# A chained attention and two gated FFNs: the second-last phase's out projection by seven quarter products, and the second FFN's input parts formed from the first one's output tiles

## The chip, the cores and the metric

One core of a Trainium2 chip. The metric is the device time of one execution in microseconds, the median of several runs.

## What is computed

```python
kv = einsum('bhsd,bhse->bhde', k, v)          # 8 x 8 x 576 x 64, float32
out = einsum('bhsd,bhde->bhse', q, kv)
x = out / sqrt(mean(out * out, -1) + 1e-6) * g_norm    # -> (4608, 512)
y = (sigmoid(x @ w_gate) * (x @ w_val)) @ w_out        # d_ff 1536
g = y @ w2_gate
z = (g * sigmoid(g) * (y @ w2_val)) @ w2_out           # (4608, 512)
```

All of it is float32; attention is linear, and two gated FFNs follow it.

## The kernel before

**Precision.** Every large product is made of rounded pieces (fp32r): an operand is split into a high part (a ScalarE copy) and a low part (a subtraction), and three products of the parts are added in PSUM. Weights are rounded and split on the chip as well; `rounded` (L377) is a chain of six operations, one on ScalarE and five on VectorE.

**Phases.** The 4608 tokens are nine blocks of 512 (`NBLK`). The hidden width of 1536 is twelve chunks of 128; a phase takes six of them for one FFN through all nine blocks. Phases 0 and 1 are FFN 1, phases 2 and 3 are FFN 2 (`PH`). In phase 0 the attention runs beside the first FFN's first half, in plain form. Phases 1 to 3 take the chunks in pairs, three steps a block (27 steps a phase), and make the gate and value products from seven quarter products instead of eight (`gv_win`, L686): 84 matmuls of 256 columns a step. The seven operands of x and of the weights (three quarters and four combinations of quarters, each in two parts) have to be formed first.

**Out products.** In phases 0 to 2 a step's out product is plain: 24 matmuls of 512 columns (`part_win`, L842), done after the next step's gv product. Only phase 3 (`WOUT`, L334) uses seven quarter products there too (`out_win`, L852): four products "early" after each step (24 matmuls of 256 columns), and three "late" ones over all three steps at the end of a block (54 matmuls). That needs h in seven operands: 11, T1, T3, T2 into two alternating places (`h_places`, L675), 21, 22, T4 into a place for each step. Each is a ScalarE copy and a GpSimd subtraction (`put`).

**x.** `x_steps` (L590) loads a block's x in four quarters of 256 KB, forms the seven operands (seven ScalarE copies, three VectorE and four GpSimd subtractions, four VectorE differences) one block ahead. Blocks alternate between a right-hand place and the arena on the left. FFN 1's output goes to DRAM (`xd[1, j]`, called yd in the trace) from `evac` (L991) in phase 1 and is loaded again in phase 2. There `keep` (L636) stores the fourteen parts of each block to `xc` in DRAM. Phase 3 loads these parts piece by piece into one place as the products of the last step before free them (`x_load`, L571, called in `product`, L721).

**Weights.** `stage` (L440) rounds a later phase's weights, forms their seven operands and stores them to `wd` in DRAM; `stage_pair` does the same for phase 3's out weights. `place` (L552) loads them in the last block before a phase, as the place of the old ones comes free (`put_place`, L1102).

**Order.** The order of PE, ScalarE, VectorE and GpSimd is written out by hand. Between products stands `tick()` (L1088; ten ticks a step), which takes thunks from queues: `att` attention, `xq` x steps, `kq` parts to keep, `wq` weights, `pq` staging. A queue paces its items by their due times (`Queue`, L1035). Phase 1's weights are staged until block 7 of phase 0, phase 2's in phase 1, phase 3's in phase 2 (`STAGED`, L1146). SP issues nearly all DMAs, in program order.

```python
721    def product(a, b, ps=None, more=False):
728        for e, w in enumerate(ws):
729            for n, (l, r) in enumerate(terms):
730                for kk in range(2):
731                    nc.tensor.matmul(ps[:, e], w[:, l, kk], xs[r // 5][:, r % 5, kk], ...)
732        if ph in WOUT and m + 2 == PH[ph][1] + PH[ph][2] and j + 1 < NBLK:
733            x_load(ph, j + 1, b)
```

Of the kernel before, what the change touches and what calls it, by code (L numbers as in the profile page):

```python
# [20 lines left out]
def attention_two_ffn(ctx: ExitStack, tc: tile.TileContext, q, k, v, g_norm, weights, out):  # L21
# [13 lines left out]
    P = 128  # L35
# [24 lines left out]
    H_AT, ARENA_AT, X_AFTER = 4 * LINE, LINE, 7 * LINE  # L60
    RIGHT, LEFT = {(1, 0): (0, LINE)}, {2: 4 * LINE}
    FIRST = {(0, 0): 5 * LINE}
# [10 lines left out]
    def open_left():  # L73
        lo_ctx.close()
        late["L"] = ctx.enter_context(tc.tile_pool(name="late_l", bufs=1, reuse_waits="tile"))
        for m in range(PH[1][1] + 2, PH[1][1] + 6):
            w_tile(0, m, 0)
        late["arena"] = shifted(late["L"], 11 * KB, F32R, ARENA_AT, "arena")

# [25 lines left out]
    for j in range(NBLK):  # L105
# [3 lines left out]
        xd[1, j] = dr.tile([P, KD, NB], F32, name=f"yd{j}")  # L109
# [224 lines left out]
    WOUT = (3,)  # L334
# [8 lines left out]
    def nop():  # L343
        pass

# [12 lines left out]
    def w_tile(f, m, c):  # L358
        d = wo if c == 2 else wgv
        if (f, m) not in d:  # L360
            ph, s = phase_of[f, m]
            pool = w0p if ph == 0 else late["R" if s < NRIGHT else "L"]
            if c == 2 and ph in WOUT:
                a = 3584 * (s // 2)
# [12 lines left out]
    def rounded(f, m, c, buf):  # L377
# [62 lines left out]
    def stage(f, m):  # L440
# [7 lines left out]
        e = m % 2  # L448
        paired = phase_of[f, m][0] in WOUT
# [18 lines left out]
        l0, o0, s0 = rounded(f, m - e, e, buf)  # L468
        l1, o1, s1 = rounded(f, m - e + 1, e, buf)
        l2, o2, s2 = rounded(f, m, 2, buf)  # L470
# [32 lines left out]
        if paired:  # L503
            return parts[0] + [parts[1][0], nop, nop] + parts[1][3:] + th + (stage_pair(f, m, buf, store, fl, hi, lo) if e else [])
# [10 lines left out]
    def stage_pair(f, m, buf, store, fl, hi, lo):  # L515
        Q, E = 2 * P, 14 * 2 * P
        l0, o0, s0 = rounded(f, m - 1, 2, buf)
        l1, o1, s1 = rounded(f, m, 2, buf)
# [14 lines left out]
        return [l0, l1, nop, nop] + o0 + o1 + [  # L533
# [18 lines left out]
    def place(f, m):  # L552
# [11 lines left out]
        return load_gv, load_o  # L564

# [10 lines left out]
    def x_tiles(ph, j):  # L576
        if (ph, j) not in xt:
            if PH[ph][3]:
                s = "RL"[((ph - 1) * NBLK + j) % 2]
                if ph in WOUT and j:  # L580
                    xt[ph, j] = x_tiles(ph, 0)
                elif s == "L":
                    xt[ph, j] = [late["arena"][:, i * 5 * DM:min(i * 5 + 5, 14) * DM].rearrange("p (c k a) -> p c k a", k=2, a=HB) for i in range(3)]
                else:
                    xt[ph, j] = [shifted(late[s], (10 - i // 2 * 2) * HB, F32R, (0, X_AFTER * (i // 2)), f"x{i}", f"x{i}").rearrange("p (c k a) -> p c k a", k=2, a=HB) for i in range(3)]
# [4 lines left out]
    def x_steps(ph, j):  # L590
# [20 lines left out]
        if ph in WOUT:  # L611
            return [lambda b=b: x_load(ph, j, b) for b in range(7)]

# [10 lines left out]
        def W(i, n, o, eng=nc.vector):  # L624
            return lambda: eng.tensor_tensor(out=X(o + 7), in0=st[i, n], in1=X(o).bitcast(F32), op=ALU.subtract)

        def D(o, a, b):
            return lambda: sub(st[o], st[a], st[b])
# [7 lines left out]
    def keep(ph, j, i):  # L636
        if j not in xc:
            xc[j] = dr.tile([P, 14 * DM], F32, name=f"xc{j}")
        t = x_tiles(ph, j)[i // 5][:, i % 5].rearrange("p k a -> p (k a)")
        nc.sync.dma_start(out=xc[j][:, i * DM:(i + 1) * DM], in_=t.bitcast(F32))  # L640
# [6 lines left out]
    h_all = shifted(hp_, 12 * HB, F32R, H_AT, "h").rearrange("p (b e s a) -> p b e s a", b=2, e=2, s=3)  # L647
    hp_.tile([P, 7 * LINE], F32, name="gap")
# [26 lines left out]
    def h_places():  # L675
        if not hw:
            raw = [wk.tile([P, 4, HB], F32R, tag="raw", name="he") for _ in range(2)]
            own = [shifted(late["R"], 4 * HB, F32R, w_shift(1, i, 2), "he", f"wo{i}").rearrange("p (c a) -> p c a", a=HB) for i in range(2)]
            hw["E"] = raw, own
            flat = h_all.rearrange("p a b c d -> p (a b c) d")  # L680
            far = [wk.tile([P, 2, HB], F32R, tag="xl", bufs=3, name="hl") for _ in range(3)]
            hw["L"] = [[flat[:, 6 * p + 2 * i:6 * p + 2 * i + 2] for i in range(3)] for p in range(2)] + [far]
            hw["n"] = 0
        return hw
# [600 lines left out]
```

## Time and profile before

| | us |
|---|---|
| median of 3 runs | 1784.44 (1781.6 to 1785.17) |
| the profiled execution, its time | 1781.64 |
| its span, first to last instruction | 1779.9 |
| PE busy | 1757.9 (99%) |
| DVE, ACT, POOL busy | 1060.0, 660.7, 683.2 |
| first gv product of phase 1, 2, 3 (chain of waits) | 549.9, 958.44, 1371.07 |

The profile shows one execution. The span leaves out what lies before the first and after the last instruction. PE's matmuls are pipelined, so busy time is no measure of its own limit. In the trace a matmul group is named by output and operands: `gv` is a gate/value product, `o` an out product, `he`, `h`, `hl` are the places of h's parts. `L341` and `L338` are the helpers `add` and `sub`.

### The profile page before, as it was taken

To read this page: it belongs to the slowest core of one execution; us is meant where nothing else is said; L and a number is where in the kernel's file an instruction comes from. 1 tells how busy PE (TensorE), PEld (TensorE's weight loads), DVE (VectorE), ACT (ScalarE), POOL (GpSimd) and SP (SyncE) were. 2 spreads that over 40 slices of the span, in tenths; PEclk is the share of its full clock that TensorE was granted. 3 is DMA by queue.
4 is the path that set the end of the run, shared out by engine and by line. 5 is a ranking of instruction groups with operands and counts; after the bars stand their busy time and mean duration, and the time that the engine had idled before them with its cause. 6 is when DMAs were issued, how large, how long until landed. Compare 5 with 4: busy or idle time off the path is not lost.

```text
span 1779.9 us, 31991 instructions
## 1 busy us (share of the span) xinstructions
PE 1757.9 (99%) x12358; PEld 1616.1 (91%) x12358; DVE 1060.0 (60%) x1754; ACT 660.7 (37%) x1349; POOL 683.2 (38%) x748
## 2 busy tenths in 40 slices
PE   7899999999999999999999999999999999999998
PEld 6788888888889999999999999999999999999998
DVE  6766566654335667676666666655553555555555
ACT  4664233333233333333333443443432433333332
POOL 1654445431012443343433444343441344444444
PEclk9999999999999999999999999999999999999999
DMA  9958796456336533434349855555568644343442
GB/s 286 285 164 230 221 227 161 132 142 237 106 108 257 187 129 103 142 107 137 125 145 397 294 188 183 185 190 189 190 237 313 214 131 131 131 131 131 131 131 72
DMA packets 274825, 320.40 MB, mean 180 GB/s; under 512 B 95856, under 2 KB 193392, under 8 KB 271984
## 3 DMA queue, kind: packets, MB, share of 16 engines
q1 hardware_dynamic: 259504, 305.24, 52.9%
q10 hardware_dynamic: 15168, 13.11, 2.4%
q8 instruction: 97, 1.59, 0.4%
q14 instruction: 56, 0.46, 0.1%
HBM read 191.14 MB, written 127.14 MB: 179 GB/s over the span
## 4 chain that ended last, share of the span: by engine, by line
PE 92%; DVE 3%; DMA 2%; issue 1%; ACT 1%; SPq 1%; POOL 1%; DVEq 0%; ACTq 0%
PE gv L731 43%; PE o L842 16%; PE gv L660 15%; PE o L828 8%; PE o L863 7%; PE ops L221 1%; PE kvps L171 1%; DMA raw<-in_moe_w_out_dram 0%; DMA qm<-in_q_dram 0%; PE xTp L268 0%; DVE u L341 0%; DVE pl L341 0%; SPq L118 0%; DMA pl<-pd 0%; DVE u L400 0%
## 5 line engine op out<-in xcount | busy, mean ns | idle before, releaser
L731 PE MATMUL gv<-x,wgv 128*128 128x256 f32 x4536 | 539.7, 279 | 0.4 <-DVE v L341 0.3
L731 PEld LDWEIGHTS gv<-x,wgv 128*128 128x128 f32 x4536 | 535.9, 188 | 3.2 <-DVE v L341 0.8
L660 PE MATMUL gv<-x,wgv 128*128 128x512 f32 x1296 | 313.8, 393 | 3.5 <-ACT x L275 2.4
L660 PEld LDWEIGHTS gv<-x,wgv 128*128 128x128 f32 x1296 | 240.3, 188 | 53.5 <-ACT x L275 2.9
L731 PEld LDWEIGHTS gv<-arena,wgv 128*128 128x128 f32 x2268 | 268.8, 188 | 3.0 <-DVE v L341 0.7
L731 PE MATMUL gv<-arena,wgv 128*128 128x256 f32 x2268 | 269.8, 279 | 0.1
L341 DVE TENSOR_TENSOR u<-u,gv 128x512 f32<-128x512 f32 x162 | 110.9, 684 | 244.8 <-PE gv L731 232.8
L719 POOL TENSOR_TENSOR h<-v,h 128x512 fp32r<-128x512 f32 x54 | 75.0, 1389 | 235.8 <-ACT h L715 235.6
L828 PE MATMUL o<-h,wo 128*128 128x512 f32 x648 | 161.9, 394 | 0.3 <-DVE h L338 0.3
L704 ACT ACTIVATE w<-v 128x256 f32<-128x256 f32 x81 | 33.9, 419 | 307.0 <-DVE v L341 307.0
L828 PEld LDWEIGHTS o<-h,wo 128*128 128x128 f32 x648 | 120.0, 188 | 25.1 <-DVE h L338 0.7
L719 POOL TENSOR_TENSOR h<-w,h 128x512 fp32r<-128x512 f32 x54 | 70.6, 1307 | 131.9 <-ACT h L715 129.9
L668 DVE TENSOR_TENSOR sg<-sg,gv 128x512 f32<-128x512 f32 x54 | 37.0, 684 | 112.1 <-PE gv L660 112.0
L842 PE MATMUL o<-h,arena 128*128 128x512 f32 x432 | 101.4, 390 | 0.0
L842 PE MATMUL o<-arena,h 128*128 128x512 f32 x432 | 101.4, 390 | 0.0
L842 PEld LDWEIGHTS o<-h,arena 128*128 128x128 f32 x432 | 79.8, 188 | 15.9
L842 PEld LDWEIGHTS o<-arena,h 128*128 128x128 f32 x432 | 79.8, 188 | 15.9
L775 POOL TENSOR_TENSOR he<-w,he 128x256 fp32r<-128x256 f32 x27 | 20.0, 742 | 182.1 <-ACT he L774 154.7
L863 PE MATMUL o<-arena,he 128*128 128x256 f32 x648 | 82.2, 281 | 0.0
L704 ACT ACTIVATE v<-g 128x256 f32<-128x256 f32 x81 | 33.9, 418 | 128.8 <-DVE g L341 128.8
L341 DVE TENSOR_TENSOR g<-u,gv 128x512 f32<-128x512 f32 x81 | 55.6, 687 | 41.4 <-PE gv L731 40.1
L863 PEld LDWEIGHTS o<-arena,he 128*128 128x128 f32 x648 | 79.0, 189 | 0.0
(145 smaller groups left out, 2601.0 us busy)
## 6 DMA issues: line engine op xcount, KB each, us to landing
wgv<-wd SPq DMA_DIRECT2D x18, 1792.0 KB, 10.0
x<-xc SPq DMA_DIRECT2D x126, 256.0 KB, 4.2
pl<-pd SPq DMA_DIRECT2D x80, 256.0 KB, 4.1
pd<-ye SPq DMA_DIRECT2D x72, 256.0 KB, 2.8
xc<-arena SPq DMA_DIRECT2D x70, 256.0 KB, 3.5
wd<-raw SPq DMA_DIRECT2D x63, 256.0 KB, 3.0
xc<-x SPq DMA_DIRECT2D x56, 256.0 KB, 3.6
raw<-in_moe_w_gate_dram SPq DMA_DIRECT2D x24, 512.0 KB, 4.6
```

Source lines behind the costliest of these rows:

```text
L171: nc.tensor.matmul(kvps[b][e * D:(e + 1) * D, hp, :D], lt, rt, start=(r == hp == 0), stop=(r == R and hp == NP - 1), skip_group_check=True)
L221: nc.tensor.matmul(ps[:, hp, :], t[:, hp, :], kvbd[2 * bp + (i > R)][:, hp, :], start=True, stop=True)
L341: nc.vector.tensor_tensor(out=out, in0=a, in1=b, op=ALU.add)
L660: nc.tensor.matmul(ps, w[:, e, a, kk, :], x[b][:, kk, :], start=(n == 0), stop=(n == 3 * KD - 1))
L668: nc.vector.tensor_tensor(out=sg, in0=sg, in1=bank[1], op=ALU.mult)
L704: nc.scalar.activation(o, t[:, 0], AF.Silu if f else AF.Sigmoid)
L719: nc.gpsimd.tensor_tensor(out=t[:, 1], in0=v, in1=t[:, 0].bitcast(F32), op=ALU.subtract)
L731: nc.tensor.matmul(ps[:, e], w[:, l, kk], xs[r // 5][:, r % 5, kk], start=(fresh and e == n == kk == 0), stop=(not more and e == 1 and n = ...
L775: nc.gpsimd.tensor_tensor(out=hs[z][:, 1], in0=x, in1=hs[z][:, 0].bitcast(F32), op=ALU.subtract)
L828: nc.tensor.matmul(ps, l, r, start=(fresh and t == 0), stop=(last and t == 2))
L842: nc.tensor.matmul(ps, l, r, start=(fresh and e == t == 0), stop=(last and e == 1 and t == 2))
L863: nc.tensor.matmul(ps[:, t], h[:, r, cs], w[:, Ax[a] + 7 * l], start=(start and t == n_ == 0), stop=(stop and t == 1 and n_ == 2), skip_gr ...
```

## The change

- `WOUT` becomes (2, 3). Phase 2's out products are formed as phase 3's are; `first_sums` adds them up into tiles and stores the partial sums. Phase 3's out weights are loaded by `place_seven`, the early pieces after each step of phase 2's last block, the late ones after the block.
- In phase 1 `evac` adds the out product to the partial sums in halves of 256 columns, and `comp_steps` forms FFN 2's x parts from these tiles and stores them to `xc`, from a new place `spare`; `yd`, `keep` and phase 2's `x_steps` go. Block 8's parts are formed in phase 2's first block, in the `xl` buffers. Every block of phases 2 and 3 loads its parts by `x_load`.
- The staging of phases 2 and 3 has a queue `rq` with due times in shares: half of phase 2's by the end of phase 0, the rest by block 5 of phase 1; a quarter of phase 3's before phase 2, the rest in phase 2. It rests from 12 ticks before phase 2 to 42 after its start. In it the last addition of `rounded` and the low parts go from VectorE to GpSimd.
- A tick takes at most one queued VectorE operation inside a gv product and two between out parts.
- h's 11 parts are issued before the seventh product, T1 to T2 after the first out part (`mid_h`), with tiles g, w0 and v in place of `ta` and `tb`. The alternating h places use `spare` in place of `raw` buffers.
- wgv is loaded in four pieces. Some addresses shift.

```diff
-    WOUT = (3,)
+    WOUT = (2, 3)
...
-    def rounded(f, m, c, buf):
+    def rounded(f, m, c, buf, eng=nc.vector):
...
         def o7():
-            add(st["u"], st["u"], st["s"])
-        return load, [o1, o3, o4, o5, o6, o7], st
+            eng.tensor_tensor(out=st["u"], in0=st["u"], in1=st["s"], op=ALU.add)
+        return load, [o1] + [V(z) for z in (o3, o4, o5, o6)] + [V(o7) if eng is nc.vector else o7], st
...
+        late_eng = nc.gpsimd if phase_of[f, m][0] > 1 else nc.vector
...
-        def lo(o, x, h, eng=nc.vector):
+        def lo(o, x, h, eng=late_eng):
...
         def load_gv():
-            nc.sync.dma_start(out=t, in_=wd[f, m][:, :E])
+            for a in range(0, E, E // 4):
+                nc.sync.dma_start(out=t[:, a:a + E // 4], in_=wd[f, m][:, a:a + E // 4])
...
+    def place_seven(f, m, what):
+        Q, E = 2 * P, 14 * 2 * P
+        for a, b in ((0, 1), (3, 6)) if what == "early" else ((1, 3), (6, 7)):
+            for l in range(2):
+                a_, b_ = a + 7 * l, b + 7 * l
+                t = w_tile(f, m, 2)[:, a_:b_].rearrange("p q a -> p (q a)").bitcast(F32)
+                nc.sync.dma_start(out=t, in_=wd[f, m][:, E + a_ * Q:E + b_ * Q])
...
-                if ph in WOUT and j:
-                    xt[ph, j] = x_tiles(ph, 0)
+                if ph in WOUT:
+                    xt[ph, j] = x_tiles(WOUT[0] - 1, NBLK - 1)
...
-    def keep(ph, j, i):
...
+    def comp_steps(j, st, buf):
+        z, th = {}, []
+        xc[j] = dr.tile([P, 14 * DM], F32, name=f"xc{j}")
+        def store(o):
+            nc.sync.dma_start(out=xc[j][:, o * DM:(o + 1) * DM], in_=z[o].rearrange("p k a -> p (k a)").bitcast(F32))
+        def H(i, n, o):
+            def run():
+                z[o] = buf()
+                nc.scalar.activation(z[o], st[i, n], AF.Copy)
+                store(o)
+            return run
+        def W(i, n, o, eng=nc.vector):
+            def run():
+                z[o + 7] = buf()
+                eng.tensor_tensor(out=z[o + 7], in0=st[i, n], in1=z[o].bitcast(F32), op=ALU.subtract)
+                store(o + 7)
+            return V(run) if eng is nc.vector else run
+        def D(o, a, b):
+            return V(lambda: sub(st[o], st[a], st[b]))
+        po = nc.gpsimd
+        return [H(0, 0, 0), W(0, 0, 0), D((0, 0), (0, 1), (0, 0)), H(1, 1, 2), W(1, 1, 2), D((0, 1), (1, 1), (0, 1)), H(0, 0, 3), W(0, 0, 3, po), nop, D((0, 0), (1, 1), (0, 0)),
+                H(0, 1, 5), W(0, 1, 5, po), nop, H(1, 0, 1), W(1, 0, 1), D((1, 0), (1, 0), (0, 0)), H(0, 0, 4), W(0, 0, 4, po), nop, H(1, 0, 6), W(1, 0, 6, po)]
...
-            if ph in WOUT and m + 2 == PH[ph][1] + PH[ph][2] and j + 1 < NBLK:
-                x_load(ph, j + 1, b)
+            after = (ph, j + 1) if j + 1 < NBLK else (ph + 1, 0)
+            if after[0] in WOUT and m + 2 == PH[ph][1] + PH[ph][2]:
+                x_load(*after, b)
...
+            def mid_h():
+                sub(g[:, 0], v[:, 0], w0[:, 0])
+                put("T1", g[:, 0])
+                sub(g[:, 1], v[:, 1], v[:, 0])
+                put("T3", g[:, 1])
+                sub(w0[:, 0], v[:, 1], g[:, 0])
+                put("T2", w0[:, 0])
 
             def late_h():
                 gated(w0[:, 1], w0[:, 1], u)
-                sub(tb[:, 1], w0[:, 1], ta[:, 1])
+                sub(v[:, 0], w0[:, 1], w0[:, 0])
                 put("22", v[:, 1])
                 put("21", w0[:, 1])
-                put("T4", tb[:, 1])
+                put("T4", v[:, 0])
...
+            def y4():
+                late("12", "21", st["c1"], all_m, False)
+                t = tile_("yt")
+                nc.scalar.activation(t, st["c1"], AF.Copy)
+                done(t, 0, 0)
+            def y5():
+                p = ps_o.tile([P, 2, HB], F32, tag="o", name="o")
+                late("S4", "22", p, all_m, True)
+                add(st["g"], st["g"], p)
+                done(st["g"], 0, 1)
+            def y6():
+                late("22", "T4", st["c7"], all_m, False)
+                add(st["u"], st["u"], st["c7"])
+                done(st["u"], 1, 0)
...
+        if ph + 1 == WOUT[0]:
+            a, k = divmod(i, 2)
+            for n in range(2):
+                t = part[ph, j, 2 * a + n]
+                add(t[:, k], t[:, k], ps[:, n * HB:(n + 1) * HB])
+            if i == 1:
...
+                th = comp_steps(j, {divmod(z, 2): part.pop((ph, j, z)) for z in range(4)}, buf)
+                for k, z in enumerate(th):
+                    kq.put(now[0] + (1 if j + 1 < NBLK else 13) + (0.75 if j + 1 < NBLK else 0.6) * k, [z], j)
+            return
...
+                if paced and t in on_vector:
+                    if not budget[0]:
+                        self.credit += n - z
+                        return
+                    budget[0] -= 1
...
-        if not first and not 0 <= now[0] - tick_of(1, 0, 0) < 13:
-            pq.pace(dt)
+        if not first and not 0 <= now[0] - tick_of(1, 0, 0) < 13 and not (-12 <= now[0] - tick_of(2, 0, 0) < 42 and rq.whole()):
+            (rq if pq.at == len(pq.items) else pq).pace(dt)
...
+    SHARES = {2: ((tick_of(1, 0, 0) - 1, 0.5), (tick_of(1, 5, 0), 1)), 3: ((tick_of(2, 0, 0) - 14, 0.25), (tick_of(2, NBLK - 1, 0) - 2, 1))}
...
+                    if j:
+                        kq.need(j - 1)
                     for z in range(4):
                         load_part(ph, j, z)
```

## Rows read from the trace of the kernel before

**Rows 1.** The page: busy us, share of the span, instructions, by engine

```profile
PE 1757.9 (99%) x12358; PEld 1616.1 (91%) x12358; DVE 1060.0 (60%) x1754; ACT 660.7 (37%) x1349; POOL 683.2 (38%) x748
```

**Rows 2.** Windows: length, busy us of PE, PEld, DVE, ACT, POOL; clock, DMA, GB/s

```profile
441.00:545.00 104.00, 104.00 (x461) 86.11 (x460) 42.73 (x66) 31.08 (x55) 10.92 (x10) 1.00 0.30 102
549.90:958.44 408.54, 408.00 (x2894) 382.06 (x2894) 276.48 (x440) 148.59 (x298) 155.91 (x125) 1.00 0.47 160
958.44:1371.07 412.63, 412.63 (x2918) 386.36 (x2918) 242.42 (x393) 163.40 (x324) 162.93 (x134) 1.00 0.63 224
1386.34:1740.91 354.57, 354.57 (x3027) 354.57 (x3026) 201.48 (x365) 116.11 (x298) 151.30 (x185) 1.00 0.42 136
```

**Rows 3.** The chain in order of time, phase 2: start us, us, what

```profile
1050.33 9.80 PE gv L731 x84
1060.13 5.47 PE o L842 x24
```

**Rows 4.** The chain in order of time, a block of phase 3

```profile
1396.15 2.80 PE o L863 x24
...
1408.74 2.88 PE o L863 x24
...
1422.12 8.51 PE o L863 x72
```

**Rows 5.** Timeline of POOL, DVE and PE in phase 3: start us, us

```profile
1486.63 1.02 POOL L775 TENSOR_TENSOR he<-ta,he 128x256 fp32r<-128x256 f32 x1 [0.88 <-ACT he L774]
...
1490.58 0.73 POOL L775 TENSOR_TENSOR h<-tb,h 128x256 fp32r<-128x256 f32 x1
...
1486.29 0.41 DVE L338 TENSOR_TENSOR ta<-v,ta 128x256 f32<-128x256 f32 x1
...
1487.07 0.86 DVE L338 TENSOR_TENSOR tb<-w,ta 128x256 f32<-128x256 f32 x1
...
1493.29 0.69 DVE L341 TENSOR_TENSOR v<-g,gv 128x512 f32<-128x512 f32 x1 [0.77 <-PE gv L731]
...
1487.43 9.96 PE L731 MATMUL gv<-x,wgv 128*128 128x256 f32 x84
```

**Rows 6.** Lines of the whole trace: busy us, mean ns of one

```profile
L341 DVE TENSOR_TENSOR u<-u,s 128x512 f32<-128x512 f32 x72 | 54.2, 753 | 1.0
...
L625 POOL TENSOR_TENSOR arena<-xl,arena 128x512 fp32r<-128x512 f32 x36 | 49.9, 1394 | 41.2 <-ACT arena L622 41.2
...
L477 POOL TENSOR_TENSOR s<-u 128x256 f32<-128x256 f32 x36 | 30.5, 848 | 117.8 <-DVE u L341 111.3 <-issue 5.2 <-PE o L842 1.4
...
L466 POOL TENSOR_TENSOR s<-s,raw 128x512 fp32r<-128x512 f32 x21 | 28.1, 1337 | 33.9 <-issue 31.4 <-POOL h L719 0.7 <-POOL x L625 0.7
...
L466 DVE TENSOR_TENSOR raw<-u,raw 128x512 fp32r<-128x512 f32 x33 | 25.9, 786 | 10.8 <-ACT raw L463 10.6
...
L466 DVE TENSOR_TENSOR raw<-u,raw 128x256 fp32r<-128x256 f32 x21 | 11.1, 528 | 3.2 <-ACT raw L463 3.2
```

**Rows 7.** Windows of 5 us at two starts of a phase

```profile
1371.00:1376.00 5.00, 5.00 (x45) 5.00 (x44) 1.32 (x2) 1.24 (x2) 1.30 (x1) 1.00 1.03 439
948.00:953.00 5.00, 5.00 (x44) 4.99 (x43) 4.65 (x8) 1.45 (x3) 1.34 (x1) 1.00 1.00 422
```

**Rows 8.** DMA issues: engine, count, KB each, median us to landing

```profile
wgv<-wd SPq DMA_DIRECT2D x18, 1792.0 KB, 10.0
x<-xc SPq DMA_DIRECT2D x126, 256.0 KB, 4.2
...
yd<-pl SPq DMA_DIRECT2D x36, 256.0 KB, 2.9
xl<-yd SPq DMA_DIRECT2D x36, 256.0 KB, 3.9
```

**Rows 9.** Waits on SP: who, for whom, us in total, times, longest

```profile
SPq L457 <- ACT raw L463: 62.3, 12, 17.9
```

More of the change, by code (lines that the diff above doesn't have):

```diff
@@ L584, in x_tiles @@
                 else:
-                    xt[ph, j] = [shifted(late[s], (10 - i // 2 * 2) * HB, F32R, (0, X_AFTER * (i // 2)), f"x{i}", f"x{i}").rearrange("p (c k a) -> p c k a", k=2, a=HB) for i in range(3)]
+                    xt[ph, j] = [late[s].tile([P, 5 - i // 2, 2, HB], F32R, tag=f"x{i}", name=f"x{i}") for i in range(3)]
             else:
@@ L673, in attention_two_ffn, with h_places @@
     hw = {}
-    def h_places():
+    def h_places(p, first):
         if not hw:
-            raw = [wk.tile([P, 4, HB], F32R, tag="raw", name="he") for _ in range(2)]
+            raw = [late["spare"][:, 4 * i:4 * i + 4] for i in range(2)]
             own = [shifted(late["R"], 4 * HB, F32R, w_shift(1, i, 2), "he", f"wo{i}").rearrange("p (c a) -> p c a", a=HB) for i in range(2)]
-            hw["E"] = raw, own
+            hw["E"] = own, raw
             flat = h_all.rearrange("p a b c d -> p (a b c) d")
-            far = [wk.tile([P, 2, HB], F32R, tag="xl", bufs=3, name="hl") for _ in range(3)]
-            hw["L"] = [[flat[:, 6 * p + 2 * i:6 * p + 2 * i + 2] for i in range(3)] for p in range(2)] + [far]
+            hw["L"] = [[flat[:, 6 * z + 2 * i:6 * z + 2 * i + 2] for i in range(3)] for z in range(2)]
             hw["n"] = 0
+        if p == 2 and first:
+            while not rq.whole():
+                rq.run(1)
+            hw["far"] = [wk.tile([P, 2, HB], F32R, tag=t, name="hl") for t in "usu"]
+        elif p == 2 and len(hw["L"]) == 2:
+            hw["L"].append([wk.tile([P, 2, HB], F32R, tag="xl", bufs=3, name="hl") for _ in range(3)])
         return hw
@@ L758, in gv_win @@
         gate(v[:, 0], g)
-        for _ in range(3):
-            tick()
-        ahead()
-        product("22", "T4", c7)
-        gated(v[:, 0], v[:, 0], g)
         if ph in WOUT:
-            pl = h_places()
             p = (m - PH[ph][1]) // 2
-            E, Lt = pl["E"][pl["n"] % 2], pl["L"][p]
+            pl = h_places(p, (ph, j) == (WOUT[0], 0))
+            E, Lt = pl["E"][pl["n"] % 2], (pl["L"] + [pl.get("far")])[p]
             pl["n"] += 1
@@ L878, in out_win @@
         all_m = range(m0, m0 + n, 2)
+        w_need((f, m0, "late"))
         st = {}
@@ L986, in load_part @@
     def load_part(ph, j, i):
+        if ph + 1 == WOUT[0]:
+            t = part[ph, j, i] = wk.tile([P, 2, HB], F32, tag="ye", bufs=4, name="pl")
+            a, n = divmod(i, 2)
+            nc.sync.dma_start(out=t, in_=pd[ph - 1, j][:, 2 * a:2 * a + 2, n * HB:(n + 1) * HB])
+            return
         if not starts(ph) or in_halves(ph, j):
@@ L1054, in pace @@
             self.credit -= n
-            self.run(n)
-    att, wq, pq, xq, kq = Queue(), Queue(), Queue(), Queue(), Queue()
+            self.run(n, True)
+    att, wq, pq, rq, xq, kq = [Queue() for _ in range(6)]
     def put_direct(f, ms, due):
@@ L1086, in w_need, with tick @@
         wq.need(key)
-    def tick(dt=1.0):
+    def tick(dt=1.0, room=9):
         now[0] += dt
+        budget[0] = room if now[0] > tick_of(1, 0, 0) else 99
         att.pace(dt)
@@ L1168, in finish @@
             p()
+            if z == 0 and rest:
+                rest[0]()
             if z == len(parts) - 1 and rest:
-                rest()
+                rest[1]()
             if n_ticks - done >= len(parts) - z:
-                tick(dt)
+                tick(dt, 2)
                 done += 1
```

149 lines of the change are left out of this document (93 added, 56 removed).

## Prediction

> **What bounds the kernel now.** I read the page first: TensorE is busy for 99% of the span, VectorE for 60%, GpSimd for 38% [rows 1]. A busy TensorE says little by itself, so I next cut the span into its phases [rows 2]. The reader is to see that in phases 2 and 3 the busy time of PE is the length of the stretch, and in phase 1 within 0.54 us of it, at a granted clock of 1.00. Then I read the chain of waits in order of time. In phase 2 a step is a gate/value product of 9.80 us and an out product of 5.47 us, with nothing between them [rows 3]. Phase 2's stretch is 412.63 us [rows 2], and 27 x (9.80 + 5.47) is 412.3 us. So 0.3 us is lost in all of it, and TensorE's own work is the length of that phase. An edit there pays by the matmul time that it removes, and costs only where it makes PE wait.
>
> Phase 1 loses a little: 27 x 9.80 + 26 x 5.47 = 406.8 us against a stretch of 408.54 [rows 2, 3], so 1.7 us.
>
> **The change, part by part.**
>
> (a) *Seven quarter products for phase 2's out.* Removed: 24 matmuls of 512 columns in each of 27 steps, 5.47 us a step, 16.4 us a block. Added: 24 matmuls of 256 columns in each step and 54 more at a block's end, 126 a block. Phase 3 does exactly this now, so its price is in the trace: 2.80 to 2.88 us for 24, 8.51 us for 72 [rows 4]. I take the whole block, since it holds the seams: phase 3's eight blocks took 354.57 us, 44.32 each; phase 2's nine took 412.63, 45.85 each [rows 2]. Per block 1.53 us, over nine blocks **-13.8 us**. Phase 1's last out product and the end of the kernel keep their form. The upper end is the matmul intervals alone: 126 x 9.80/84 = 14.70 us against 16.41, so 1.71 x 9 = 15.4 us; the lower is 13.5 (the chain's 45.82 for three steps against 44.32). I take 13.8, the measured period.
>
> The row shows 117 ns for a matmul of 256 columns and 228 ns for one of 512. The Trainium skill (TensorE: Matmul & The Clock Gate, section Back-to-back issue gap) gives 262 and 518 cycles, 109 and 216 ns at 2.4 GHz; by that the gain would be 72 x 216 - 126 x 109 = 1.8 us a block, an estimated 16.3 us in all. The measured durations are longer and decide.
>
> (b) *What stands beside it in phase 2.* Phase 3's h parts (seven ScalarE copies and seven GpSimd subtractions a step) come to phase 2. GpSimd pays 18.9 us a block at most (151.30 / 8, with phase 3's own sums in it [rows 2]). Three quarters of phase 3's staging also lies here, 2.25 pairs of weight chunks. A pair costs GpSimd about 33 us: 12 sums of 0.85, six splits of 1.34 as now, six final adds moved from VectorE (I take the split's 1.34), and splits moved from VectorE, three of 1.34 and three of 0.85 [rows 6]. So 170 + 2.25 x 33 + 5 for the last block's x parts (four splits of 1.39 [rows 6]) = 249 us of some 399: 62%, against 162.93 of 412.63 now [rows 2]. VectorE loses 36 x 0.75 + 18 x 0.79 + 18 x 0.53 = 51 us of staging [rows 6] and all of phase 2's x forming, and gains four subtractions of h a step; it stays near its 59%.
>
> What hides GpSimd's work, and how much can it hide? In phase 3 the last subtraction of a step (T4's low half) ends at 1490.58 + 0.73 = 1491.31. After the change its source is the tile that the next step's `v` goes into, and `v` is now written at 1493.29: 2.0 us of cover. Behind `v` stands the step's seventh product, which adds to the bank that `v` reads. It starts six products of 1.40 us after 1487.43, at 1495.83, while `v` is done at 1493.98: 1.9 us more [rows 5]. So PE waits only when GpSimd runs over 3.9 us late. Staging is 74 us over some 22 steps, 3.4 us a step, and not all of it falls into that window. But it comes in bunches: four sums in a row are 3.4 us, with one split 4.7. I take half a microsecond of wait in four of the 22 steps: **+2 us**, bounds 0 and 9 (half of the steps 0.8 us).
>
> (c) *Phase 1: x parts for FFN 2 formed here.* VectorE takes over three splits and four differences a block for eight blocks, and eight additions of 256 columns where there were four of 512; it sheds some of the staging. From 276.48 us of 408.54 (68%) it goes to some 71%. The new limit of one queued VectorE operation a tick spreads them. Behind each stand the additions that free the gv banks. SP loses the 36 x loads through `yd` (3.9 us to land [rows 8]) and as many stores, keeps the 14 `xc` stores a block, now out of a ring of four buffers, and gains 126 more `xc` loads in phase 2. Two waits are new on SP: a store of a part waits for its GpSimd or VectorE split, and the four partial-sum loads of a block wait until the x steps of the block before are through. Behind them in SP's order stand x loads for the next block, due a step later, and weights. I take **+0.5 us** beside the 1.7 us now lost; bounds -1.7 (all of that goes) and +5.
>
> (d) *The boundaries.* At the two starts of phases 2 and 3, the first block's x (14 x 256 KB = 3.67 MB) now comes piece by piece during the last step before, beside that step's wgv (two of 1792 KB). The queues already run full there: 422 and 439 GB/s [rows 7]. Work it out for phase 3's start, the tighter: the first wgv begins 2.87 us before the last gv, the second goes behind two x pieces, place_seven's 1 MB behind four. At 430 GB/s the queue is through some 17 us after that gv's start, plus about 4 us to land [rows 8]. The last x piece is wanted by the new block's seventh product, 12.7 + 9 us after: about even. The pieces ahead of it have more room. **+0.5 us**, bounds 0 and 8. SP's own order matters here: it has waited 17.9 us at one staging store [rows 9], but around phase 2's start staging rests.
>
> (e) *Half of phase 2's staging in late phase 0.* 1.5 pairs, 50 us of GpSimd, into a stretch of 104 us where GpSimd is busy for 10.92, VectorE for 42.73 and DMA for 0.30 [rows 2]. Nothing, bounds 0 and 1. Loading wgv in quarters and the shifted addresses: three more SP issues a chunk, no bytes more; nothing.
>
> **The sum.** The profiled execution took 1781.64 us, 1779.9 of them span. -13.8 + 2 + 0.5 + 0.5 = -10.8, so 1770.8 on its own basis. The median of the three runs is 2.8 us above it, which would give 1773.6. I forecast **1772 us**.
>
> **The rivals.**
>
> *Boundary data late.* All x of a first block waits behind weights: 3.67 MB at 430 GB/s is 8.5 us, at two boundaries; half of it exposed at both is 8.5 us more: 1780. For it: the full queues [rows 7]. Against: phase 3 loads x piecewise between its own blocks and its period is even. Chance 0.10.
>
> *VectorE bunches in phase 1.* x parts not finished by a block's last step are run all at once: 21 steps in a row, 11 on VectorE or GpSimd at 0.8 to 1.4 us. At 1.2 us of PE wait in eight blocks, +9.6: 1781, no change. For it: PE already loses 1.7 us in this phase. Against: 17 ticks of due time where 18 pass. Chance 0.10.
>
> *GpSimd becomes the bound in phase 2 (slower).* If each of the 22 steps with staging meets a bunch plus an operation blocked by one more split of 1.34 us [rows 6], the delay is 4.7 + 1.3 us against a cover of 3.9, 2.1 us a step: 46 us at most; at half of that, 23 us, the time is 1781.6 - 13.8 + 23 = 1791. It decides once the average loss passes 0.8 us a step. Against: the mean load of 3.4 us a step lies below the cover. For it: VectorE and GpSimd stretch one another. VectorE's subtraction of 0.41 us took 0.86 beside a GpSimd one, and that one 1.02 where it takes 0.73 alone [rows 5]. The Trainium skill (SBUF — State Buffer, section Who interferes with whom) calls this an exclusive lock: a VectorE operation with two SBUF inputs and a GpSimd one that reads SBUF block each other for a whole instruction. By that a meeting can cost up to a whole GpSimd split, three times the 0.45 us that the row's VectorE operation lost; the row bears out the lock, not that length. Chance 0.10.
>
> *Forecast,* 0.66, with 0.04 for more gain (phase 1's losses gone: 1766). That (a) does not do what it says I rule out: phase 3 shows its price.
>
> **How the numbers follow.** A measurement of this kernel can tell about 0.2%, 3.6 us: faster is below 1780.9, slower above 1788. Forecast and extra gain, 0.70, are faster; of the boundary rival 0.07 and of phase 1's rival 0.04; the rest of these two, 0.09, with 0.01 of the GpSimd rival, is the same; 0.09 is slower. So 0.81, 0.10, 0.09. The range 1765 to 1782 takes in the bounds of each term alone and the first two rivals, and leaves the GpSimd rival out; the forecast's own is 1766 to 1777.
>
> **What would show it.** Phase 2 from first gv to first gv near 399 us instead of 412.63, with 44.3 us a block, phase 3 as before. GpSimd near 60% in phase 2; PE waits there on `v` if (b) is too small. At the first gv of phases 2 and 3 PE waiting for a DMA of x would show (d). Phase 1 longer than 410 us would show (c). A phase 2 above 410 us proves the forecast wrong.

## The result, and the profile after

The changed kernel is slower: 1795.95 us, the median of four runs, against 1783.17 for the kernel before, which now has four runs too; the ratio is 1.0071, 95% interval 1.0053 to 1.0088. The forecast was 1772, range 1765 to 1782. The profiled execution has a span of 1794.2 us, 14.3 more than before.

The page's first row and the windows of the changed kernel stand against [rows 1, 2]. The windows are late phase 0, phase 1, phase 2 and eight blocks of phase 3.

```profile
PE 1755.4 (98%) x12844; PEld 1635.8 (91%) x12844; DVE 1168.4 (65%) x1871; ACT 685.6 (38%) x1472; POOL 875.6 (49%) x973
```

```profile
441.00:545.00 104.00, 104.00 (x460) 86.12 (x460) 54.37 (x73) 38.98 (x70) 49.25 (x43) 1.00 0.44 145
548.73:964.55 415.82, 410.20 (x2893) 383.92 (x2892) 334.18 (x483) 171.28 (x348) 254.05 (x195) 1.00 0.61 210
964.55:1372.31 407.76, 400.02 (x3350) 396.29 (x3349) 266.27 (x454) 157.78 (x386) 215.38 (x251) 0.99 0.57 200
1395.74:1755.34 359.60, 355.23 (x3026) 353.65 (x3026) 214.82 (x368) 117.02 (x296) 150.93 (x184) 1.00 0.42 137
```

TensorE's busy time fell by 2.5 us while the span grew, so time was lost in gaps, and in a lower clock behind some of them (below). The stages place it. Phase 0 ends 1.0 us earlier (548.73 against 549.74, the start of PE's first gv product of phase 1 in its timeline; the chain of waits has 549.90). Phase 1 takes 415.8 us where it took 408.5, phase 2 407.8 where it took 412.6. Eight blocks of phase 3 take 359.60 where they took 354.57: 44.95 us each instead of 44.32. In the forecast phase 2 was to take 399 and phase 3 was not to change.

To see single waits I took the start of each gv product from PE's timeline, so each step has a length. With nothing to wait for, a step of phase 1 takes 15.27 us (9.80 + 5.47), a step of phase 2 or 3 now takes 12.61 (9.80 + 2.80), and the step in which the last block's late products run takes 18.91. What is above these is lost:

| where | steps, us | lost |
|---|---|---|
| phase 1, 2nd step | 19.93 | 4.7 |
| phase 1, 15th and 16th step | 17.57, 16.97 | 4.0 |
| phase 2, 1st step | 16.97 for 15.27 | 1.7 |
| phase 2, 3rd and 4th step | 19.15, 20.43 | 8.1 |
| phase 2, first steps of later blocks | 18.91 to 20.16 | 4.5 |
| phase 3, 1st step | 23.26 | 4.4 |
| phase 3, first steps of the eight later blocks | 19.74 | 6.6 |

That is 33.9 us, against 3.4 us of the same kind before (1.6 in phase 1, 0.3 in phase 2, 1.5 in phase 3's eight blocks). The waits of PE in the changed kernel name what came last in each (who, for whom, us in total, times, longest):

```profile
PE gv L775 <- ACT u L783: 4.7, 3, 2.0
PE gv L775 <- DMA x<-xc: 4.4, 6, 2.7
PE o L909 <- DVE g L341: 4.4, 8, 0.6
...
PE gv L775 <- DMA wgv<-wd: 2.5, 2, 1.8
...
PE gv L775 <- DVE v L341: 1.4, 1, 1.4
```

Their sum is smaller than the table's, in part because some waits are also paid in a slower clock behind them (below). Before the change there is one such row after phase 0, 0.3 us.

**Phase 1's second step: SP's order.** SP's timeline at the end of phase 0, before the change:

```profile
541.78 0.89 SPq L558 DMA_DIRECT2D wgv<-wd  x2
```

and after it:

```profile
537.57 4.75 SPq L464 DMA_DIRECT2D wd<-raw  x2
...
542.91 1.46 SPq L464 DMA_DIRECT2D wd<-raw  x3
...
547.26 1.12 SPq L394 DMA_DIRECT2D raw<-in_moe_w_val_dram  x2
...
549.44 5.35 SPq L567 DMA_DIRECT2D wgv<-wd  x8
```

Line 558, now 567, loads phase 1's second pair of weights. It used to go out at 541.78 us. Now it goes out at 549.44, behind staging stores (L464) that wait for GpSimd and ScalarE. PE wants them for the phase's second gv product, which would start at 558.5. What the wait then costs is to be seen in windows of 4 us (length, busy us of PE, PEld, DVE, ACT, POOL, granted clock, DMA share, GB/s):

```profile
556.00:560.00 4.00, 3.40 (x30) 3.19 (x28) 2.32 (x5) 1.71 (x4) 0.27 (x1) 1.00 1.03 417
560.00:564.00 4.00, 2.13 (x12) 1.93 (x13) 1.21 (x1) 1.26 (x3) 2.28 (x2) 0.90 1.05 398
564.00:568.00 4.00, 4.00 (x26) 4.00 (x25) 1.14 (x2) 0.00 (x0) 0.00 (x0) 0.68 1.04 380
568.00:572.00 4.00, 4.00 (x36) 4.00 (x35) 2.00 (x5) 0.74 (x2) 0.00 (x0) 1.00 1.03 402
```

PE is busy for 2.13 of 4 us from 560, and in the next 4 us, busy all the time, it is granted 0.68 of full speed: part of that stretch at the lower level of 1.2 GHz. The granted shares of 0.90 and 0.68 over 4 us each are some 1.7 us of PE's time, beside the 2.5 us of waiting; together they are most of the 4.7.

**Phase 2's third and fourth step: a ring of three.** ScalarE's timeline in phase 2's first block:

```profile
997.18 0.63 ACT L663 ACTIVATE xz<-pl 128x512 fp32r<-128x512 f32 x1 [5.55 <-DMA xc<-xz]
...
1001.96 0.58 ACT L783 ACTIVATE u<-gv 128x512 f32<-128x512 f32 x1
...
1019.12 0.63 ACT L663 ACTIVATE xz<-pl 128x512 fp32r<-128x512 f32 x1 [2.35 <-DMA xc<-xz]
1019.66 0.58 ACT L783 ACTIVATE u<-gv 128x512 f32<-128x512 f32 x1
```

and PE's there:

```profile
1002.59 2.21 PE L775 MATMUL gv<-x,wgv 128*128 128x256 f32 x12 [2.01 <-ACT u L783]
...
1020.29 3.08 PE L775 MATMUL gv<-x,wgv 128*128 128x256 f32 x24 [1.24 <-ACT u L783]
```

`xz` are the last block's x parts on their way to DRAM, in three buffers. The copies at 997.18 and 1019.12 had to wait for a store from the buffer that they take. SP's timeline shows these stores:

```profile
976.60 4.70 SPq L567 DMA_DIRECT2D wgv<-wd  x4
982.14 0.32 SPq L571 DMA_DIRECT2D arena<-wd  x1
...
986.76 1.49 SPq L658 DMA_DIRECT2D xc<-xz  x2
...
1011.28 2.88 SPq L658 DMA_DIRECT2D xc<-xz  x2
1014.50 0.95 SPq L592 DMA_DIRECT2D x<-xc  x2
```

The first went out at 986.76 behind 3584 KB of weights and had not landed by 996. The second went out from 1011.28 on, among the next block's x loads (L592). The copy of `gv` at 1019.66 (L783), on which the additions that free PSUM banks depend, is behind the copy at 1019.12 in ScalarE's order, and PE resumes at 1020.29.

**Phase 3's first step: x behind weights.** SP's timeline at the seam:

```profile
1363.54 2.13 SPq L567 DMA_DIRECT2D wgv<-wd  x4
1365.77 1.13 SPq L592 DMA_DIRECT2D x<-xc  x2
1367.09 3.48 SPq L582 DMA_DIRECT2D arena<-wd  x4
1371.43 6.82 SPq L592 DMA_DIRECT2D x<-xc  x8
```

Four of the seven pairs of x pieces go out at 1371.43 or later, behind the second step's weights (L567) and phase 3's early out weights (L582).

```profile
1379.40 5.83 PE L775 MATMUL gv<-x,wgv 128*128 128x256 f32 x36 [2.72 <-DMA x<-xc]
```

**Phase 3's blocks: VectorE's order.** The chain of waits at a block's end, where [rows 4] show 8.51 us of out products without a gap:

```profile
1477.22 0.69 DVE u L341
1478.54 1.06 issue
1479.60 0.96 DVE w L338
1480.56 0.61 DVE g L341
1481.19 1.23 DVE pl L341
1482.51 0.70 DVE g L341
1483.25 2.39 PE o L909 x18
```

The difference `w` (L338, in `mid_h`) and its wait lie ahead of the sum `g` (L341). Before the change the three differences of h came ahead of the first sum of the out products. Now they stand between the first and the second, and the last sum, on which the bank for the late products depends, comes 0.55 us too late, in eight blocks (4.4 us in the row above). At their new place the second and third difference also take 1.52 and 0.96 us, beside operations of GpSimd; in the run that moves them back (the first experiment) they take 0.42 each.

### The profile page after: what moved, and what is told of

It is laid out like the page before. It is cut to its first block, busy times and chain, and to the rows that moved or that the text cites. A ratio compares the mean times of both kernels' runs of the same rounds, so it can differ in the third digit from the quotient of the medians.

```text
span 1794.2 us, 33872 instructions
## 1 busy us (share of the span) xinstructions
PE 1755.4 (98%) x12844; PEld 1635.8 (91%) x12844; DVE 1168.4 (65%) x1871; ACT 685.6 (38%) x1472; POOL 875.6 (49%) x973
## 5 line engine op out<-in xcount | busy, mean ns | idle before, releaser
L775 PE MATMUL gv<-x,wgv 128*128 128x256 f32 x5796 | 699.9, 281 | 13.6 <-DMA x<-xc 4.4
L775 PEld LDWEIGHTS gv<-x,wgv 128*128 128x128 f32 x5796 | 690.4, 190 | 17.9 <-issue 4.3
L699 PEld LDWEIGHTS gv<-x,wgv 128*128 128x128 f32 x1296 | 241.4, 189 | 53.6 <-ACT x L275 2.8
L341 DVE TENSOR_TENSOR u<-u,gv 128x512 f32<-128x512 f32 x162 | 110.7, 683 | 136.8 <-PE gv L775 105.4
L748 ACT ACTIVATE w<-v 128x256 f32<-128x256 f32 x81 | 33.9, 418 | 292.2 <-DVE v L341 278.0
L775 PEld LDWEIGHTS gv<-arena,wgv 128*128 128x128 f32 x1008 | 119.5, 188 | 2.7 <-ACT u L783 1.6
L775 PE MATMUL gv<-arena,wgv 128*128 128x256 f32 x1008 | 120.0, 280 | 1.4 <-ACT u L783 1.4
L815 POOL TENSOR_TENSOR he<-w,he 128x256 fp32r<-128x256 f32 x54 | 41.5, 769 | 148.7 <-ACT he L814 148.7
L815 POOL TENSOR_TENSOR spare<-w,spare 128x256 fp32r<-128x256 f32 x54 | 41.1, 761 | 147.6 <-ACT spare L814 144.5
L909 PE MATMUL o<-arena,h 128*128 128x256 f32 x636 | 84.2, 282 | 5.5 <-DVE g L341 4.4
L416 POOL TENSOR_TENSOR u<-u,s 128x512 f32<-128x512 f32 x36 | 50.2, 1395 | 75.1 <-DVE s L413 63.5
L341 DVE TENSOR_TENSOR v<-g,gv 128x512 f32<-128x512 f32 x81 | 55.6, 686 | 44.9 <-PE gv L775 41.5
L909 PE MATMUL o<-arena,spare 128*128 128x256 f32 x648 | 81.5, 280 | 0.0
L748 ACT ACTIVATE v<-g 128x256 f32<-128x256 f32 x81 | 33.9, 419 | 124.2 <-DVE g L341 124.2
```

What stands on the lines that cost most here:

```text
L341: nc.vector.tensor_tensor(out=out, in0=a, in1=b, op=ALU.add)
L416: eng.tensor_tensor(out=st["u"], in0=st["u"], in1=st["s"], op=ALU.add)
L699: nc.tensor.matmul(ps, w[:, e, a, kk, :], x[b][:, kk, :], start=(n == 0), stop=(n == 3 * KD - 1))
L748: nc.scalar.activation(o, t[:, 0], AF.Silu if f else AF.Sigmoid)
L815: nc.gpsimd.tensor_tensor(out=hs[z][:, 1], in0=x, in1=hs[z][:, 0].bitcast(F32), op=ALU.subtract)
L909: nc.tensor.matmul(ps[:, t], h[:, r, cs], w[:, Ax[a] + 7 * l], start=(start and t == n_ == 0), stop=(stop and t == 1 and n_ == 2), skip_gr ...
```

## The experiments

Executions differ in phase 0 by up to 6 us: in the changed kernel and in three runs whose edits do not touch phase 0, phase 1 begins at 548.73, 549.48, 551.78 and 554.48 us. So beside the time I read the steps. All ratios are to the kernel before the change.

**h's T parts first.** In `finish`:

```diff
-            p()
             if z == 0 and rest:
                 rest[0]()
+            p()
```

> T1 and T3 of h are formed ahead of the first out part again (as before the change), not behind it. Theory A (order): a block of phase 3 took 44.95 us after the change and 44.32 before it, because at a block's end VectorE runs the three h differences between the sums of the second and the third quarter product, and the bank of the S4 product comes free late. Then a block of phase 3 falls to 44.3 to 44.4 us (9 blocks: about 5 us), phase 2 loses 1 to 2 us more, and the whole is 5 to 7 us shorter than the changed kernel's 1795.95 (1789 to 1791). Rival B (GpSimd and VectorE stretch each other): the tiles that h's differences now share with g, w0 and v make the wait; then the block stays at 44.9 to 45.0 and the time within 1.5 us of 1796.

1791.05 us, ratio 1.0049 (1.0033 to 1.0065); the profiled execution was the slowest of six, 1798.46. Phase 3's blocks take 44.13 us, each first step 18.91:

```profile
1484.67 8.40 PE o L909 x72
```

72 matmuls in 8.40 us, no gap. That is 0.8 us a block less than with the change and 0.2 less than before it: the part of `mid_h` that uses g, w0 and v does no harm, only its place did. Phase 2 did not gain the 1 to 2 us expected: it took 411.1 us, 3.3 longer: 1.6 in the two steps of the ring (17.94 and 23.23 us), 1.1 in the first steps of later blocks, 0.7 in its first step. Its losses have other causes.

**Staging rests before phase 1.**

```diff
-    2: ((tick_of(1, 0, 0) - 1, 0.5), ...
+    2: ((tick_of(1, 0, 0) - 12, 0.5), ...
-    not 0 <= now[0] - tick_of(1, 0, 0) < 13
+    not -11 <= now[0] - tick_of(1, 0, 0) < 13
```

> Phase 2's first half of staging is due 12 ticks before phase 1 instead of 1, and staging rests from 11 ticks before it. Theory A (SP's order): the changed kernel lost about 4.6 us in phase 1's first two steps because SP stood at staging stores (wd from raw) while phase 1's second pair of weights waited behind them: the first of these went out at 549.4 us, before the change at 541.8. Then they go out by 543, PE waits for no weights there, phase 1's first two gv products take 19.6 to 20 us instead of 24.2, and the whole is 3.5 to 5 us shorter. Rival C (DMA bandwidth): the four-piece loads and the spare place make these loads late whatever SP does; then the stall stays above 3 us.

1800.0 us, ratio 1.01 (1.0071 to 1.0129): longer, where 3.5 to 5 us less was expected. Phase 1's second step takes 15.28 us. But its weights went out at 552.55 us, not by 543, and were in time because phase 1 began only at 559.9, 5 to 11 us later than in the four starts above. So this run does not by itself show that SP's order was the cause; the last one below does. The same staging pressed into 11 ticks less stalls phase 0; three rows of the waits from 490 to 555 us in this run:

```profile
POOL u L416 <- DVE s L413: 22.7, 3, 8.9
...
ACT u L470 <- POOL raw L473: 11.0, 3, 5.7
...
PE o L874 <- ACT h L353: 5.1, 2, 3.2
```

ScalarE, in order, stood up to 5.7 us at high parts whose place GpSimd's low parts (L473) still read, and the h copies of phase 0 (L353), for which PE waited 5.1 us, stood behind it. I had not expected that.

**Seven buffers for the last block's parts.**

```diff
-    return wk.tile([P, 2, HB], F32R, tag="xl", bufs=3, name="xz")
+    k = ring[0] % 7
+    ring[0] += 1
+    if k < 3:
+        return wk.tile([P, 2, HB], F32R, tag="xl", bufs=3, name="xz")
+    if k % 2:
+        more[0] = wk.tile([P, 4, HB], F32R, tag="raw", name="xy")
+    return more[0][:, 0:2] if k % 2 else more[0][:, 2:4]
```

> The x parts of FFN 1's last block go through a ring of seven buffers (the three xl ones and two raw buffers in halves) instead of three. Theory A (ring behind a full queue): in phase 2's first block ScalarE and VectorE stood in order at a part whose buffer waited for its store, which stood behind weights in SP's queue, and PE lost about 8 us in the second and third step (16.35 us for a gv product instead of 9.80, then 1.5). With seven buffers the second step's gv product takes 9.8 to 12 us and the whole is 5 to 8 us shorter. Rival B (GpSimd and VectorE stretch each other, too many operations in that block): the stall stays at 5 us or more, since not an operation goes.

1789.88 us, ratio 1.0043 (1.0023 to 1.0062). PE's timeline in the same stretch:

```profile
996.97 9.97 PE L775 MATMUL gv<-x,wgv 128*128 128x256 f32 x84
1006.77 2.96 PE L909 MATMUL o<-arena,spare 128*128 128x256 f32 x24
1009.57 8.86 PE L775 MATMUL gv<-x,wgv 128*128 128x256 f32 x72
```

The third step takes 12.60 us instead of 19.15, phase 2 400.1 instead of 407.8. Theory A holds for the third step: not an operation less, and its stall of 6.5 us is gone. The fourth still takes 20.28 us where it took 20.43; PE waits there for x pieces now (0.74 us) and no longer for ScalarE.

**x first at the seams.**

```diff
-    put_place(ph + 1, i, 0, 6)
+    put_place(ph + 1, i, 0, 16 if i == 2 and ph + 1 in WOUT else 6)
-    wq.put(now[0] + 4, [lambda fm=fm, z=z: place_seven(..., "early")], ...)
+    wq.put(now[0] + 12, [lambda fm=fm, z=z: place_seven(..., "early")], ...)
```

> In the last block before phases 2 and 3 the second step's weights are due 16 ticks on instead of 6, and phase 3's early out weights 12 instead of 4, so that the next block's x parts go ahead of them in SP's order. Theory A (place in the queue): phase 3's first gv product lost 4.4 us and phase 2's 1.7 us to x parts behind 3 to 4 MB of weights; both fall to 0.5 us or less, the whole is 4 to 6 us shorter. Rival C (bandwidth): the bytes at the seam are what cannot be moved in time; then the wait only moves to the weights of the second step or to the out weights, and the whole is within 1.5 us of 1796.

1795.47 us, ratio 1.0075 (1.0045 to 1.0104): nothing, at first sight. By the steps both stalls shrank as theory A has it (phase 2's first step 15.27 us, phase 3's 19.49 instead of 23.26, 0.6 above 18.91), and the ring's stall was 10.8 us; it is 8.1 in the changed kernel and 8.9 to 9.7 in three other runs with three buffers and without this edit. ScalarE's first wait for a buffer there grew from 5.55 to 7.60 us; that the weights now ahead of its stores are the reason is likely, not shown. With the later start of phase 1 in this execution (551.78) that hides the gain.

**The three together.** The edits of the first, third and fourth run.

> The first, third and fourth edits together (h's T parts first, seven buffers for the last block's x parts, x before weights at the seams); staging stays as in the changed kernel. Theory A (separate causes, they add): phase 3's blocks 44.1 us, its first gv step and phase 2's first without a wait for x, phase 2's second and third step without the ring's stall, which the fourth edit alone made worse (42.3 us for the two against 39.6): phase 2 about 396 to 399 us, phase 3 to the last matmul 407 us, the whole 1779 to 1783, about the time before the change. Rival B (the engines beside PE are too full): the stalls come back elsewhere in phase 2, which stays at 404 us or more, and the whole at 1786 or more.

1780.73 us, ratio 0.9988 (0.9977 to 0.9999). Phase 2 takes 400.1 us and phase 3 to its last matmul 406.5, as the separate causes have it (phase 2 stayed 1 us above the range given). Phase 1, which none of the three touches, still takes 417.3.

**Staging on VectorE again**, with the three edits:

```diff
-    late_eng = nc.gpsimd if phase_of[f, m][0] > 1 else nc.vector
+    late_eng = nc.vector
```

(and the same in `stage_pair`).

> As the run with three edits, and staging's last addition and low parts back on VectorE, as before the change. In phase 1 the changed kernel loses 4 us in two steps (17.57 and 16.97 us instead of 15.27), where ScalarE stood in order behind a GpSimd bunch of seven staging operations. Theory D (the move to GpSimd makes that wait): both steps are at 15.3 to 15.6, and phase 1 is 3 to 4 us shorter than with three edits. Rival E (the x parts that phase 1 now forms fill VectorE): VectorE gets 51 us of work back over phases 0 to 2, the two steps stay above 16.5 or others take their place, and phase 1 is as long or longer.

1771.97 us, ratio 0.9945 (0.9922 to 0.9968). Phase 1 takes 410.3 us. The two steps in its middle take 15.94 and 15.28 us, and its second step 16.35 where it took 21.51: from 528 to 562 us SP's staging stores waited 5.6 us for GpSimd, and now 0.6 in the like stretch. Theory D holds in its direction; phase 1 is 7.0 us shorter, not 3 to 4, because of the second step, which it did not count, one of the two steps stays above 15.6, and the eighth and ninth step now lose 1.6 us.

The edit alone, on the changed kernel:

> The changed kernel with one edit: staging's last addition and low parts on VectorE, as before the change. With the three other edits this took 8.8 us off (1780.7 to 1772.0), 7.0 of them in phase 1. Theory D (the move to GpSimd has its own price): alone it takes off 7 to 10 us as well, 1786 to 1789; phase 1 at 409 to 411 us, its steps of 17.57 and 16.97 us below 16. Rival G (it pays only where the other waits are gone, through shared slack): 3 us or less, 1793 to 1796.

1789.78 us, ratio 1.0031 (1.0021 to 1.0042): 6.2 us shorter, a little under the 7 to 10 of theory D; phase 1 takes 410.7 us, its two steps 15.92 and 15.27. So most of the price does not hang on the other waits.

Only the low parts on VectorE, with the three edits:

> The three edits, and of staging only the low parts on VectorE; its last addition stays on GpSimd. Theory D1 (ScalarE's order: it stands at a high part whose buffer GpSimd's low part still reads): the low parts carry the loss, phase 1 comes to 410 to 412 us and the whole to 1772 to 1775. Rival D2 (GpSimd's share of time, and VectorE stretched beside it, whichever operations they are): the 36 additions of 1.4 us are the larger part, phase 1 stays at 413 to 416 and the whole at 1776 to 1779.

1773.46 us, ratio 0.9949 (0.9934 to 0.9964), phase 1 410.6: the low parts carry 7.3 of the 8.8 us. But D1's reason is only a part of it. The 16th step, where ScalarE stood behind GpSimd, went from 16.99 to 15.27, and that is 1.7 us; 4.9 us came from phase 1's second step (21.51 to 16.59), through SP. The 15th step stayed at 17.46: it goes only with the additions.

**Staging in its old phases.** All of phase 2's in phase 1 and phase 3's in phase 2 (with the three edits, on GpSimd; then on VectorE):

```diff
-    SHARES = {2: (..., 0.5), (tick_of(1, 5, 0), 1)), 3: (..., 0.25), (tick_of(2, NBLK - 1, 0) - 2, 1))}
+    SHARES = {2: ((tick_of(1, NBLK - 1, 0) - 2, 1),), 3: ((tick_of(2, NBLK - 1, 0) - 2, 1),)}
...
-            (rq if pq.at == len(pq.items) else pq).pace(dt)
+            (rq if now[0] > tick_of(1, 0, 0) else pq).pace(dt)
```

> As the run with three edits, and phase 2's staging all in phase 1 and phase 3's all in phase 2, as before the change; nothing of it in phase 0. Theory A: no staging store stands before phase 1's weights on SP, so phase 1's first two steps take 9.8 and 15.3 us instead of 9.8 and 19.9 (4.6 us less); phase 0 is no longer. In exchange phase 1 holds six weight chunks of staging beside the x parts: VectorE at some 75% and GpSimd some 70%; 2 to 6 us of new stalls there. Together between 3 us shorter and 2 us longer than the run with three edits. Rival F (phase 1 has room): no new stalls, 4 to 5 us shorter.

> As the run with staging in its old phases, and also on its old engines (the last addition and the low parts on VectorE). Theory D (GpSimd bunches make the stalls in phase 1): phase 1 is 2 to 5 us shorter than with GpSimd. Rival E (VectorE is the full one in phase 1, some 80%): phase 1 is 3 us or more longer than with GpSimd.

1817.47 us (ratio 1.0199, 1.0169 to 1.0228) and 1799.68 (1.0099, 1.0069 to 1.0128). Phase 1's second step is 15.27 us in both, as theory A has it, but phase 1 takes 438.5 and 425.6 us. Rival F falls: phase 1 has no room for that staging once it also forms FFN 2's x parts, as it is ordered and paced here. So moving half of it to phase 0 pays, in spite of the wait that it brings in the second step. The 2 to 6 us of new stalls that theory A gave were far too few: phase 1's steps lie 31.7 us above 406.8. VectorE is again the better place, by 12.8 us in phase 1, where theory D gave 2 to 5.

**No limit on VectorE operations** (three edits, staging on VectorE):

> The three edits and staging on VectorE, without the limit on queued VectorE operations in a tick. If the limit keeps bunches away from the additions that free PSUM banks, phase 1 (410.3 us) gets 1 to 5 us longer and phase 2 (399.2) 0 to 3. If it only delays staging, both stay within 0.5 us or get shorter by up to 1.

1791.19 us, ratio 1.0042 (1.0027 to 1.0056); phase 1 takes 424.3 us, 14 us longer, phase 2 403.2. The limit that the change brought does much more than I thought.

**Best version:** the three edits, staging on VectorE, and a rest of 5 ticks before phase 1.

> The three edits and staging on VectorE, and staging rests from 5 ticks before phase 1. Theory A (SP's order): the second step of phase 1 takes 15.3 us instead of 16.35, no new wait comes into late phase 0 since VectorE's staging does not queue behind GpSimd there (when staging on GpSimd was pressed into 12 ticks less, phase 0 lost 10 us), the whole 1770.5 to 1771.5. Rival: the pressed staging costs 1 us or more in phase 0, 1772 to 1774.

1771.78 us, ratio 0.9934 (0.9912 to 0.9957); not to be told from the run without the rest. The second step takes 15.28 us, since SP issues the weights early again, 8 us before phase 1 as in the kernel before the change:

```profile
541.20 4.13 SPq L567 DMA_DIRECT2D wgv<-wd  x8
```

and phase 0 loses nothing (phase 1 begins at 549.38). Its windows, as above:

```profile
549.38:959.23 409.85, 407.96 (x2894) 382.15 (x2892) 341.40 (x515) 171.22 (x348) 217.23 (x163) 1.00 0.60 205
959.23:1359.31 400.08, 395.80 (x3350) 393.15 (x3348) 277.06 (x478) 156.65 (x386) 189.06 (x227) 1.00 0.58 203
1378.36:1731.39 353.03, 353.03 (x3027) 353.03 (x3026) 202.02 (x368) 114.95 (x296) 150.34 (x184) 1.00 0.44 144
```

Phase 2 takes 400 us, eight blocks of phase 3 353.03, 44.13 us each. GpSimd's busy time in phase 1 is 217 us where it was 254. In phase 2 PE's steps are still 6.6 us above their sum, all of it in the first steps of blocks; I did not follow these.

## Why the prediction was wrong

**(a) held.** The quarter products removed what the trace of phase 3 said. Blocks of phase 3 with no wait take 44.13 us where phase 2's took 45.85 [rows 2]: 15.5 us over nine blocks. 13.8 was taken, with an upper end of 15.4.

**(b) failed twice.** GpSimd was weighed with care: its cover of 3.9 us before PE waits on `v`. In phase 2 no wait of PE is put down to `v`, and GpSimd was busy there for 215 us where 249 were counted. What was not weighed is what else stands in order: the last block's parts in their ring of three were costed as 5 us of GpSimd work, and the store behind each buffer not at all, although it joins the queue that term (d) had just filled: 8.1 us, of which seven buffers took off 6.7. And the new place of `mid_h` got no term: phase 3 was to stay "as before", and lost 5.0 us against it. The 4.5 us in the first steps of phase 2's later blocks had no term either. PE's waits in these steps name sums of the partial products (L341, `yt`, 1.1 us), a staging operation on VectorE (L406, 0.8) and x pieces (0.7); no run tests them, and their cause stays open.

**(c) was mis-sized.** 0.5 us was taken, bounds up to 5; 4.0 came in two steps. VectorE was to reach 71% and reached 80% (334.18 of 415.82 us), for the most part because its operations on SBUF tiles got longer beside GpSimd. The same line in phase 1 before and after (x count | busy us, mean ns):

```profile
L338 DVE TENSOR_TENSOR xl<-xl 128x512 f32<-128x512 f32 x36 | 29.0, 806 | 0.5
```

```profile
L338 DVE TENSOR_TENSOR xl<-xl 128x512 f32<-128x512 f32 x32 | 38.1, 1192 | 0.1
```

From 806 to 1192 ns. One of the longest of them, with the GpSimd operation beside it:

```profile
758.78 1.74 POOL L670 TENSOR_TENSOR spare<-pl,spare 128x512 fp32r<-128x512 f32 x1
```

```profile
759.29 1.77 DVE L338 TENSOR_TENSOR xl<-xl 128x512 f32<-128x512 f32 x1
```

The start times in the two traces divide the line. Where no GpSimd operation ran when one began, it took 686 ns on average before and 684 after. Where one ran, it took 1019 (13 of 36) and 1496 (20 of 32). I had used means of the kernel before for work in a fuller phase. The prediction cited the Trainium skill (SBUF — State Buffer, section Who interferes with whom) for a lock between the two engines as a reason for a slower outcome; these rows agree with it. But the stretch is not shown to make the 4.0 us: with staging back on VectorE the same line still takes 1227 ns and VectorE is busy for 342.17 of 410.34 us, 83%, and yet phase 1 is shorter. What is shown is that staging on GpSimd makes most of it: with staging back on VectorE in the changed kernel the two steps lose 0.7 us. In the 15th step PE waits 1.4 us for `v` on VectorE, which runs staging and x parts without a pause before it; in the 16th came a wait that I had not named, ScalarE waiting for GpSimd (ACT and POOL in the changed kernel):

```profile
784.83 0.63 ACT L470 ACTIVATE u<-s 128x512 fp32r<-128x512 f32 x1 [3.95 <-POOL raw L473]
...
785.88 0.58 ACT L783 ACTIVATE u<-gv 128x512 f32<-128x512 f32 x1
```

```profile
783.50 1.29 POOL L473 TENSOR_TENSOR raw<-u,raw 128x512 fp32r<-128x512 f32 x1
```

`u<-s` may be written only when the low part has read `u`; the copy of gv stands behind it.

**(d) was mis-sized.** 0.5 us was taken and 8 allowed; 1.7 and 4.4 came. The working followed the last x piece, found it about even, and gave the pieces ahead of it "more room". The pair that PE waited for in phase 3 is the fourth product's: it went out at 1371.43 at the earliest, behind the early out weights, was wanted at 1376.7 and held PE until 1379.40. From 1360 to 1376 us the queues moved 299 to 405 GB/s, where the working took 430.

**(e) was wrong.** Nothing was taken for half of phase 2's staging in phase 0, bounds 0 and 1. Engine shares were compared, and they had room. The question that was not asked is what stands behind the moved stores on SP: phase 1's weights, 4.7 us.

So the losses, 33.9 us, were forecast as 3 beside the 3.4 of before. The sign that was to prove the forecast wrong, a phase 2 above 410 us, did not come (407.8): 19.7 us of the loss lay in phases 1 and 3. The rival of a slower outcome (GpSimd, 0.10) had the right sign and, in part, the right engine: staging on GpSimd cost 6.2 us alone and 8.8 with the other waits gone. But it cost through SP's stores and ScalarE's order in phase 1, not through `v` in phase 2, so that its 1791 us is near the measured time is luck. The forecast of 1772 us is about the time that the change takes once four waits in order are mended, which is no merit of the forecast.

## What to carry to other kernels

Where one engine has no gaps, the time removed from it is easy to forecast and the new gaps are not: for each operation, store or load that is moved, write down what stands behind it in each in-order queue (SP's too) and when that is wanted, before comparing shares of busy time. A buffer whose release is a store is only as fast as the DMA queue in front of that store, so look at such rings where weights are being loaded. Several small orders of this kind added up to about twice the gain here, and four of them were mended by order, buffers or the choice of engine, without a change of the products.

## What the runs showed of the hardware

One wait of PE cost about twice its length, as the granted clock fell behind it: 2.5 us of waiting for weights became 4.7 us of the step, with 0.68 granted in the 4 us after it. A VectorE subtraction of two SBUF tiles (128x512, fp32) took 684 ns where no GpSimd operation ran at its start, and 1496 ns on average, up to 1779, where one did; an addition with one input in PSUM took 679 and 682 (`u<-u,gv`, phase 1 of the changed kernel). And VectorE's busy time is no fixed sum: when 51 us of staging by the forecast's count came back from GpSimd, VectorE's busy time in late phase 0 and phases 1 and 2 rose by 25.5 us (682.6 in the run with staging on VectorE, 657.1 in the one with three edits), and phase 1 got shorter.
